# Top-k attention and two expert layers: the second head's keys stored with their last 64 in front

## Chip, cores and metric

The kernel runs on one core of a Trainium2 chip. The time is the device time of one execution in microseconds: 2257.2 us, the median of three runs of the kernel before (2256.66 to 2257.63).

## What is computed

```
scores = q @ k.T / sqrt(64)              # batch 4, heads 8, 576 queries, 576 keys, head size 64
mask   = scores >= 32nd largest of the row
attn   = softmax over the kept scores
x      = attn @ v                        # then laid out as [2304, 512]
x      = ((x @ w1) * (x @ w2)) @ w3 @ w_out
P      = exp(x @ w_gate - max), 8 rounds of row and column normalization
out    = sum over 8 experts e of P[:, e] * (relu(x @ m1[e]) @ m2[e])
```

All of it is float32. Matrix products run on operands that are split into a high and a low part.

## The kernel before

576 keys are four blocks of 128 (S4 = 512) and a rest of 64 (SR). Attention runs in the first third of the time, the expert layers in the rest; the change touches attention alone. Between the attention work, products of the first expert layer (L663, L691) are put in as filler for TensorE.

**Visits and steps.** A visit is one batch, one pair of heads and a range of query blocks; there are 28, numbered from 0. In all but the first batch each head pair has two visits, of two query blocks each. Attention goes in 72 steps of about 10 us. A normal step takes one query block of both heads of the pair (j = 0 is the first head, j = 1 the second): 64 of them. Eight tail steps take the 64 last queries of both heads, for two head pairs at once; there j is the head pair.

**A step's stations.** They are spread over four consecutive steps by an order written out by hand (`ORDERS`, one letter group for each operation): scores (`st_scores`, S0 and S1, L306), a top-32 search on VectorE and GpSimd, thresholding and exponential on ScalarE, normalization on GpSimd, transposes (`st_trans`, R0 and R1: four at L415 and one at L416 for each j), a copy of the transposed weights from the PSUM tile `tx` into `et` (L418, ScalarE), and the product with v (`st_av`, A, L444). Rows 512 to 575 of the keys go through the fifth transpose; it turns the columns 448 to 575 of one head, and v's tile `vn` has zeros for the 64 keys that come a second time. `P` in the order takes one piece of the preparation of the next visit, `F` a share of the filler.

**Preparation of a visit** (`prep_list`). Queries and keys come in from HBM, are transposed on TensorE (L229), copied into `kt` or `qt` (L145, ScalarE; one buffer each), split into parts (L245 ScalarE, L246 GpSimd), and put together for the scores by DMAs from one place of SBUF to another (`prep_stack`): the keys into `kst` (two buffers; for each head one DMA of 64 partitions by 2 by 576 at L258 and two of 64 by 576 at L260, six in all), the queries into `qst` (two buffers; L266 blocks, L268 the last 64). The next visit's copy into `kt` (L145) has to wait for all DMAs that read `kt`.

**SP's queue.** All these DMAs, the loads of v (`load_v`, L135 and L138), of k and q (L125, L127) and the stores of the expert layer (L698, L700) are issued by SyncE in the order of the program; an issue that waits holds up all behind it. In most visits the order is: keys into `kst`, v, queries into `qst`, next loads.

Of the kernel before, what the change touches and what calls it, by code (L numbers as in the profile page):

```python
# [7 lines left out]
F32 = mybir.dt.float32  # L8
# [10 lines left out]
def kernel(  # L19
# [14 lines left out]
    nc = tc.nc  # L34
# [66 lines left out]
    tx = aps.tile([128, 1024], F32, name="tx")  # L101
    vn_t = [ap1.tile([128, 2 * R + 2, D], F32, name=f"vn{i}") for i in range(2)]
    qst_t = [ap1.tile([128, 2 * S4 + 256], F32R, name=f"qst{i}") for i in range(2)]
# [27 lines left out]
    def load_v(p):  # L131
        b, hp = visits[p][:2]
        t = vn_t[p % 2]
        for i in range(2):
            nc.sync.dma_start(t[:, R * i:R * i + R, 0:D],  # L135
                              v[b, 2 * hp + i, 0:S4, :].rearrange("(p r) d -> p r d", r=R))
        for i in range(2):
            nc.sync.dma_start(t[64:128, 2 * R + i, 0:D], v[b, 2 * hp + i, S4:S, :])  # L138

# [27 lines left out]
    def prep_first():  # L167
# [8 lines left out]
        for n in range(2):  # L176
            copy(kst[0, n][:, :, S4:S], pt[:, 256 + 128 * n:384 + 128 * n].rearrange("p (h r) -> p h r", h=2), nc.vector)

    def prep_group(p, nm, g, eng=None, flip=False):
# [22 lines left out]
        else:  # L202
# [6 lines left out]
            if body:  # L209
                copy(dst[:, body[0] // R, 0:S4], pt, eng)  # L210
            if tail:
                copy(dst[:, :, S4:S], pt[:, w:w + 128].rearrange("p (h r) -> p h r", h=2), eng)

# [34 lines left out]
    def prep_stack(p, nm):  # L248
# [3 lines left out]
        if nm == "k":  # L252
            ks = ap1.tile([128, 2, 2, S], F32R, name="kst", tag="kst", bufs=2)
            for n in range(2):
                kst[p, n] = ks[:, n]
            for h in range(2):
                x = hl[64 * h:64 * h + 64]
                nc.sync.dma_start(ks.bitcast(F32)[0:64, :, h], x)  # L258
                for a in range(2):
                    nc.sync.dma_start(ks.bitcast(F32)[64:128, 1 - a, h], x[:, a])  # L260
            return
# [32 lines left out]
    def st_scores(st, j):  # L294
# [9 lines left out]
        for n, (lhs, hh, part) in enumerate(terms):  # L304
            for e in range(2):
                nc.tensor.matmul(ps[:, e, 0:SH], lhs, kst[p, part][:, hh, SH * e:SH * e + SH],  # L306
                                 start=(n == 0), stop=(n == len(terms) - 1))
        if j == 0:
# [102 lines left out]
    def st_trans(st, j):  # L411
        e = e_sb[st][:, j]
        ps = tx
        for c in range(R):
            nc.tensor.transpose(ps[:, 128 * c:128 * c + 128], e[:, 128 * c:128 * c + 128], ident)  # L415
        nc.tensor.transpose(ps[:, S4:S4 + 128], e[:, S - 128:S], ident)  # L416
        et = ap1.tile([128, (R + 1) * 128], F32, name="et", tag="et", bufs=2)
        nc.scalar.activation(et, ps[:, 0:(R + 1) * 128], AF.Copy)  # L418
        et_sb[st, j] = et
        if j:  # L420
            e_sb.pop(st)

    def st_av(st):
# [3 lines left out]
        if steps1[st][0][1] is None:  # L427
            for j in range(2):
                p = steps1[st][j][0]
                for c in range(R + 1):  # L430
                    for hh in range(2):
                        nc.tensor.matmul(ps[64 * hh:64 * hh + 64, 64 * j:64 * j + 64],
                                         vn_t[p % 2][:, R * hh + c if c < R else 2 * R + hh],
                                         et[j][:, 128 * c + 64 * hh:128 * c + 64 * hh + 64],
                                         start=(c == 0), stop=(c == R))
# [6 lines left out]
        for c in range(R + 1):  # L442
            for hh in range(2):
                nc.tensor.matmul(ps[64 * hh:64 * hh + 64, 0:128],  # L444
                                 vn_t[p % 2][:, R * hh + c if c < R else 2 * R + hh],
                                 et[hh][:, 128 * c:128 * c + 128], start=(c == 0), stop=(c == R))
        b, hp = visits[p][:2]
# [1206 lines left out]
```

## Time and profile before

| | |
|---|---|
| median of three runs | 2257.2 us |
| the profiled execution: time, span | 2257.63 us, 2255.8 us |
| mean granted TensorE clock | 0.984 |
| busy share of the span: PE, DVE, ACT, POOL | 97%, 79%, 54%, 67% |
| instructions of PE and of ACT | 13521, 2708 |

PE is TensorE's matmuls (transposes among them), PEld its weight loads, DVE VectorE, ACT ScalarE, POOL GpSimd, SP SyncE, and SPq SP's queue of DMA issues. L415 is line 415 of the kernel. In a timeline a row has its start in us from the start of the span, its duration, engine, line and operation, the tile that is written and what is read; x4 means four instructions that run after and into one another, and what stands in brackets is the idle time of the engine before the row and what ended it, by the profile. Ends of matmuls are modelled; the distance from start to start is the better measure of what one costs. A wait for several semaphores is put down to the one that came last by the profile; where the engine named had long been done, it was another, often a DMA.

### The profile page before, as it was taken

The page shows a single profiled execution, that of the slowest core. Times are in us where ns is not written, and L with a number is a line of the kernel's source. Part 1 is how long each engine was busy: PE and PEld are TensorE (multiplying, and loading weights), DVE is VectorE, ACT ScalarE, POOL GpSimd, SP SyncE. Part 2 cuts the span into 40 slices and gives each one's busy share as a digit, 9 for nine tenths or more (in the row PEclk, how much of TensorE's full clock was granted, in tenths as well). Part 3 has the DMA queues.
Part 4 walks back from the last instruction along what each step waited for, and adds up shares of the span by engine and source line. Part 5 has one row for each costly group of instructions (what it writes and reads, how often), then busy time and mean ns, then how long its engine had stood idle before and what let it go on. Part 6 is the DMA issues. An engine that isn't in the chain of part 4 may idle for free.

```text
span 2255.8 us, 42437 instructions
## 1 busy us (share of the span) xinstructions
PE 2186.6 (97%) x13521; PEld 2021.9 (90%) x13521; DVE 1774.2 (79%) x4396; ACT 1220.0 (54%) x2708; POOL 1515.3 (67%) x1828
## 2 busy tenths in 40 slices
PE   5897999999999999999999999999999999999999
PEld 4554898998888999999999899999999999999999
DVE  8999999999999557777777767777777677777776
ACT  7999778877777544444444344444444433333332
POOL 6889877767776257787778667777777544444443
PEclk6998999999999999999999999999999999999999
DMA  6545444544542177788778898888888987887885
GB/s 191 154 139 135 105 105 113 124 102 103 122 112 53 60 250 241 270 301 290 248 250 295 274 319 275 277 274 280 276 279 266 349 274 252 259 258 256 260 256 161
DMA packets 356078, 485.45 MB, mean 215 GB/s; under 512 B 95152, under 2 KB 166032, under 8 KB 355856
## 3 DMA queue, kind: packets, MB, share of 16 engines
q1 hardware_dynamic: 354320, 480.71, 67.7%
q8 instruction: 108, 1.77, 0.3%
q10 hardware_dynamic: 1536, 2.03, 0.3%
q14 instruction: 114, 0.93, 0.1%
HBM read 309.48 MB, written 132.43 MB: 196 GB/s over the span
## 4 chain that ended last, share of the span: by engine, by line
PE 82%; DVE 6%; POOL 4%; ACT 4%; DMA 2%; SPq 2%; issue 1%; ACTq 0%; POOLq 0%; DVEq 0%
PE l1ps L1219 30%; PE y L1518 20%; PE y L1278 12%; PE abps L663 8%; PE x2ps L691 3%; PE sps L306 2%; PE tx L444 2%; DVE tkv L355 2%; PE tx L415 2%; POOL low L344 1%; DVE rest L360 1%; DMA kst<-kt 1%; DVE G L517 1%; ACT s_sb L396 1%; PE x2ps L689 1%
## 5 line engine op out<-in xcount | busy, mean ns | idle before, releaser
L1219 PE MATMUL l1ps<-xB,wa 128*128 128x384 f32 x2688 | 540.6, 338 | 1.0 <-DVE tm_u L1448 0.5
L1518 PE MATMUL y<-h,v 128*128 128x384 f32 x2640 | 531.6, 337 | 0.2
L1219 PEld LDWEIGHTS l1ps<-xB,wa 128*128 128x128 f32 x2688 | 475.1, 188 | 3.4 <-DVE tm_u L1448 2.3
L1518 PEld LDWEIGHTS y<-h,v 128*128 128x128 f32 x2640 | 467.6, 188 | 0.9 <-DVE h L1455 0.8
L1455 POOL TENSOR_TENSOR h<-tm_t,h 128x384 fp32r<-128x384 f32 x192 | 195.9, 1021 | 245.4 <-ACT h L1454 239.3
L1529 DVE TENSOR_TENSOR Mc<-y,Mc 128x384 f32<-128x384 f32 x424 | 234.5, 553 | 139.2 <-PE y L1518 139.0
L1278 PE MATMUL y<-wb,hh 128*128 128x512 f32 x768 | 270.4, 394 | 0.0
L1219 PE MATMUL l1ps<-xAh,wa 128*128 128x384 f32 x896 | 260.6, 338 | 0.0
L1024 POOL TENSOR_TENSOR wa<-ws,wa 128x256 fp32r<-128x256 f32 x217 | 164.8, 762 | 98.6 <-ACT wa L1023 94.0
L1287 DVE SCALAR_TENSOR_TENSOR acc<-y,P,acc 128x512 f32<-128x512 f32 x168 | 126.0, 750 | 98.8 <-PE y L1278 96.3
L1455 POOL TENSOR_TENSOR h<-tm_b,h 128x384 fp32r<-128x384 f32 x128 | 133.5, 1048 | 87.1 <-ACT h L1454 72.4
L1454 ACT ACTIVATE h<-tm_t 128x384 fp32r<-128x384 f32 x192 | 99.5, 519 | 152.9 <-DVE tm_t L1493 148.9
L332 POOL TENSOR_TENSOR low<-s_sb 128x288 int32<-128x288 int32 x144 | 117.8, 818 | 95.9 <-ACT s_sb L310 94.0
L1244 ACT ACTIVATE hh<-l1ps 128x384 fp32r<-128x384 f32 x128 | 63.0, 492 | 211.8 <-DVE l1ps L1240 120.5
L355 DVE MAX8 tkv<-rest 128x8 f32<-128x288 f32 x432 | 175.1, 447 | 0.0
L1219 PEld LDWEIGHTS l1ps<-xAh,wa 128*128 128x128 f32 x896 | 164.8, 188 | 7.8 <-issue 0.5
L1278 PEld LDWEIGHTS y<-wb,hh 128*128 128x128 f32 x768 | 144.0, 188 | 24.6
L306 PE MATMUL sps<-kst,qst 128*128 128x288 f32 x640 | 128.8, 329 | 32.5 <-DVE top L339 31.3
L1219 PE MATMUL l1ps<-xAl,wa 128*128 128x384 f32 x448 | 150.5, 336 | 0.0
L1278 PE MATMUL y<-wb,hl 128*128 128x512 f32 x384 | 149.5, 389 | 0.0
L306 PEld LDWEIGHTS sps<-kst,qst 128*128 128x128 f32 x640 | 98.8, 199 | 56.1 <-DVE top L339 44.8
L1454 ACT ACTIVATE h<-tm_b 128x384 fp32r<-128x384 f32 x128 | 66.4, 521 | 135.5 <-DVE tm_b L1451 129.8
(223 smaller groups left out, 5321.2 us busy)
## 6 DMA issues: line engine op xcount, KB each, us to landing
wa<-wk SPq DMA_DIRECT2D x448, 256.0 KB, 3.5
v<-vk SPq DMA_DIRECT2D x343, 256.0 KB, 3.9
wk<-wa SPq DMA_DIRECT2D x224, 256.0 KB, 3.0
vk<-v SPq DMA_DIRECT2D x105, 256.0 KB, 2.8
ws<-in_moe_w_dram SPq DMA_DIRECT2D x35, 512.0 KB, 5.1
vk<-sp SPq DMA_DIRECT2D x68, 256.0 KB, 3.4
raw<-in_moe_w_dram SPq DMA_DIRECT2D x32, 512.0 KB, 4.1
ws<-in_moe_w_dram SPq DMA_DIRECT2D x128, 128.0 KB, 2.7
```

Source lines behind the costliest of these rows:

```text
L306: nc.tensor.matmul(ps[:, e, 0:SH], lhs, kst[p, part][:, hh, SH * e:SH * e + SH], start=(n == 0), stop=(n == len(terms) - 1))
L332: nc.gpsimd.tensor_tensor(low_sb[st][:, j].bitcast(I32), x[:, 0:SH], x[:, SH:S], ALU.add)
L355: nc.vector.max(vt[:, j, c:c + 8], x[:, j])
L663: nc.tensor.matmul(ps[:, 0:n], lhs, rhs[:, c, 0:n], start=(m == 0), stop=(m == 3 * KD - 1))
L1024: eng.tensor_tensor(t[:, 1], st[:, c], t[:, 0].bitcast(F32), ALU.subtract)
L1219: nc.tensor.matmul(ps, lhs[:, kc], rhs[:, kc], start=(first and k_ == 0), stop=(k_ == 3 * KH - 1), skip_group_check=True)
L1278: nc.tensor.matmul(ps, lhs[:, m, h, o:o + 128], rhs[:, m], start=(k_ == 0), stop=(k_ == 5))
L1287: nc.vector.scalar_tensor_tensor(a, ps, P[:, i, e:e + 1], a, op0=ALU.mult, op1=ALU.add)
L1454: nc.scalar.activation(h[k][:, 0], src, AF.Copy)
L1455: low = lambda: eng.tensor_tensor(h[k][:, 1], src, h[k][:, 0].bitcast(F32), ALU.subtract)
L1518: nc.tensor.matmul(ps, w[:, a, 128 * j:128 * j + 128], h[:, b], start=(first and q_ == 0), stop=(q_ == 5), skip_group_check=True)
L1529: nc.vector.tensor_tensor(m, ps, m, ALU.add)
```

## The change

The second head's keys are stored with keys 512 to 575 in front of keys 0 to 511. In a normal step the last 64 columns of the first head's weights and the first 64 of the second head's then lie side by side, and one transpose turns both: R0 has four transposes, R1 five. `vn` gets the first head's last 64 rows of v in partitions 0 to 63 for this, and a third tile with the same rows in partitions 64 to 127 for the tail steps, which takes one more DMA a visit. `prep_stack` stores the second head's keys in two ranges: six DMAs where there were three. In tail steps, where both heads stand in one row, the scores of the second head are put back in the old order by cutting its second matmul in two (224 and 64 columns), ten transposes stay, and the copy of j = 0 is in two pieces. `et` is one tile for each j.

```diff
--- before.py
+++ after.py
@@ -99,7 +99,7 @@
     nat = {}
     xT = [ap1.tile([128, KD, S], F32, name=f"xT{i}") for i in range(2)]
     tx = aps.tile([128, 1024], F32, name="tx")
-    vn_t = [ap1.tile([128, 2 * R + 2, D], F32, name=f"vn{i}") for i in range(2)]
+    vn_t = [ap1.tile([128, 2 * R + 3, D], F32, name=f"vn{i}") for i in range(2)]
     qst_t = [ap1.tile([128, 2 * S4 + 256], F32R, name=f"qst{i}") for i in range(2)]
     for i in range(2):
         nc.gpsimd.memset(vn_t[i][:, 2 * R:, :], 0.0)
@@ -135,7 +135,8 @@
             nc.sync.dma_start(t[:, R * i:R * i + R, 0:D],
                               v[b, 2 * hp + i, 0:S4, :].rearrange("(p r) d -> p r d", r=R))
         for i in range(2):
-            nc.sync.dma_start(t[64:128, 2 * R + i, 0:D], v[b, 2 * hp + i, S4:S, :])
+            nc.sync.dma_start(t[64 * i:64 * i + 64, 2 * R + i, 0:D], v[b, 2 * hp + i, S4:S, :])
+        nc.sync.dma_start(t[64:128, 2 * R + 2, 0:D], v[b, 2 * hp, S4:S, :])
 
     kst = {}
     split = {}
@@ -174,7 +175,7 @@
         copy(qst_t[0][:, 0:2 * S4].rearrange("p (h s) -> p h s", h=2)[:, :, 0:128],
              pt[:, 0:256].rearrange("p (h s) -> p h s", h=2), None, scale)
         for n in range(2):
-            copy(kst[0, n][:, :, S4:S], pt[:, 256 + 128 * n:384 + 128 * n].rearrange("p (h r) -> p h r", h=2), nc.vector)
+            copy(kst[0, n].rearrange("p h s -> p (h s)")[:, S4:S4 + 128], pt[:, 256 + 128 * n:384 + 128 * n], nc.vector)
 
     def prep_group(p, nm, g, eng=None, flip=False):
 
@@ -207,9 +208,8 @@
                     kst[p, m] = ks[:, m]
             dst = kst[p, n]
             if body:
-                copy(dst[:, body[0] // R, 0:S4], pt, eng)
-            if tail:
-                copy(dst[:, :, S4:S], pt[:, w:w + 128].rearrange("p (h r) -> p h r", h=2), eng)
+                h = body[0] // R
+                copy(dst[:, h, SR * h:S4 + SR * h], pt, eng)
 
     kgroups = [list(range(R)), list(range(R, 2 * R)), [2 * R]]
 
@@ -255,9 +255,11 @@
                 kst[p, n] = ks[:, n]
             for h in range(2):
                 x = hl[64 * h:64 * h + 64]
-                nc.sync.dma_start(ks.bitcast(F32)[0:64, :, h], x)
-                for a in range(2):
-                    nc.sync.dma_start(ks.bitcast(F32)[64:128, 1 - a, h], x[:, a])
+                for s0, s1, d0 in ((0, S4, SR), (S4, S, 0)) if h else ((0, S, 0),):
+                    d1 = d0 + s1 - s0
+                    nc.sync.dma_start(ks.bitcast(F32)[0:64, :, h, d0:d1], x[:, :, s0:s1])
+                    for a in range(2):
+                        nc.sync.dma_start(ks.bitcast(F32)[64:128, 1 - a, h, d0:d1], x[:, a, s0:s1])
             return
         for h in range(2):
             for a in range(2):
@@ -302,9 +304,12 @@
             c0 = S4 * h + 128 * t
             terms = [(qs[:, c0:c0 + 128], h, part) for part in range(2)]
         for n, (lhs, hh, part) in enumerate(terms):
-            for e in range(2):
-                nc.tensor.matmul(ps[:, e, 0:SH], lhs, kst[p, part][:, hh, SH * e:SH * e + SH],
-                                 start=(n == 0), stop=(n == len(terms) - 1))
+            cuts = ((0, 0, SH, 0), (1, 0, SH, SH))
+            if h is None and hh:
+                cuts = ((0, 0, SH, SR), (1, 0, SH - SR, SH + SR), (1, SH - SR, SH, 0))
+            for e, c0, c1, k0 in cuts:
+                nc.tensor.matmul(ps[:, e, c0:c1], lhs, kst[p, part][:, hh, k0:k0 + c1 - c0],
+                                 start=(n == 0), stop=(n == len(terms) - 1), skip_group_check=True)
         if j == 0:
             s_sb[st] = ap1.tile([128, 2, S], F32, name="s_sb", tag="s_sb", bufs=4)
         nc.scalar.activation(s_sb[st][:, j].rearrange("p (a b) -> p a b", a=2), ps[:, :, 0:SH], AF.Copy)
@@ -411,11 +416,22 @@
     def st_trans(st, j):
         e = e_sb[st][:, j]
         ps = tx
+        both = steps1[st][0][1] is not None
+        c0 = SR if both and j else 0
         for c in range(R):
-            nc.tensor.transpose(ps[:, 128 * c:128 * c + 128], e[:, 128 * c:128 * c + 128], ident)
-        nc.tensor.transpose(ps[:, S4:S4 + 128], e[:, S - 128:S], ident)
-        et = ap1.tile([128, (R + 1) * 128], F32, name="et", tag="et", bufs=2)
-        nc.scalar.activation(et, ps[:, 0:(R + 1) * 128], AF.Copy)
+            nc.tensor.transpose(ps[:, 128 * c:128 * c + 128], e[:, c0 + 128 * c:c0 + 128 * c + 128], ident)
+        w = S4
+        if j or not both:
+            ends = e_sb[st].rearrange("p j s -> p (j s)")[:, S4:S4 + 128] if both else e[:, S - 128:S]
+            nc.tensor.transpose(ps[:, w:w + 128], ends, ident)
+            w += 128
+        et = ap1.tile([128, (R + j) * 128], F32, name=f"et{j}", tag=f"et{j}", bufs=1)
+        w = min(w, (R + j) * 128)
+        nc.scalar.activation(et[:, 0:w], ps[:, 0:w], AF.Copy)
+        et = [et[:, 128 * c:128 * c + 128] for c in range(R + j)]
+        if not j and not both:
+            nc.scalar.activation(e[:, 0:128], ps[:, S4:S4 + 128], AF.Copy)
+            et.append(e[:, 0:128])
         et_sb[st, j] = et
         if j:
             e_sb.pop(st)
@@ -430,8 +446,8 @@
                 for c in range(R + 1):
                     for hh in range(2):
                         nc.tensor.matmul(ps[64 * hh:64 * hh + 64, 64 * j:64 * j + 64],
-                                         vn_t[p % 2][:, R * hh + c if c < R else 2 * R + hh],
-                                         et[j][:, 128 * c + 64 * hh:128 * c + 64 * hh + 64],
+                                         vn_t[p % 2][:, R * hh + c if c < R else 2 * R + 2 - hh],
+                                         et[j][c][:, 64 * hh:64 * hh + 64],
                                          start=(c == 0), stop=(c == R))
             for j in range(2):
                 b, hp = visits[steps1[st][j][0]][:2]
@@ -443,7 +459,7 @@
             for hh in range(2):
                 nc.tensor.matmul(ps[64 * hh:64 * hh + 64, 0:128],
                                  vn_t[p % 2][:, R * hh + c if c < R else 2 * R + hh],
-                                 et[hh][:, 128 * c:128 * c + 128], start=(c == 0), stop=(c == R))
+                                 et[hh if c < R else 1][c], start=(c == 0), stop=(c == R))
         b, hp = visits[p][:2]
         xev.append(lambda: nc.scalar.activation(xT[b % 2][:, hp, 128 * t:128 * t + 128], ps[:, 0:128], AF.Copy))
 
```

## Rows read from the trace of the kernel before

**Rows 1.** Windows: length; busy us (x) PE, PEld, DVE, ACT, POOL; clock; DMA; GB/s.

```profile
40.00:240.00 200.00, 164.72 (x984) 109.58 (x984) 191.47 (x629) 189.84 (x387) 172.80 (x204) 0.88 0.52 139
240.00:720.00 480.00, 472.50 (x3921) 425.54 (x3920) 448.18 (x1666) 378.90 (x871) 348.67 (x508) 1.00 0.45 107
```

**Rows 2.** Groups by shape, 240 to 720 us: busy, mean ns, idle before.

```profile
L415 PE MATMUL tx<-ident,s_sb 128*128 128x128 f32 x402 | 60.6, 273 | 0.6 <-ACT et L418 0.5
...
L418 ACT ACTIVATE et<-tx 128x640 f32<-128x640 f32 x100 | 69.9, 699 | 11.1 <-PE tx L416 10.3
```

**Rows 3.** Timeline of PE, 404 to 407 us: start, us, what.

```profile
404.48 0.60 PE L415 MATMUL tx<-ident,s_sb 128*128 128x128 f32 x4
404.91 0.27 PE L416 MATMUL tx<-ident,s_sb 128*128 128x128 f32 x1
...
405.73 0.69 PE L306 MATMUL sps<-kst,qst 128*128 128x288 f32 x4
406.26 0.28 PE L663 MATMUL abps<-xh,w2h 128*128 128x256 f32 x1
```

**Rows 4.** Chain that ended last, 240 to 720 us: start, us, what.

```profile
278.69 3.84 DMA kst<-kt
287.35 1.83 DMA qst<-qt
```

**Rows 5.** Timeline of SP, ACT and PE, 274 to 287 us.

```profile
274.88 0.62 SPq L258 DMA_DIRECT2D kst<-kt  x1
...
277.95 1.97 SPq L260 DMA_DIRECT2D kst<-kt  x2
...
281.18 1.13 SPq L138 DMA_DIRECT2D vn<-in_v_dram  x2
...
282.40 1.07 SPq L266 DMA_DIRECT2D qst<-qt  x1
282.61 0.60 ACT L145 ACTIVATE kt<-pt 128x512 f32<-128x512 f32 x1 [0.57 <-DMA kst<-kt]
283.52 0.59 SPq L268 DMA_DIRECT2D qst<-qt  x1
283.85 1.31 PE L444 MATMUL tx<-et,vn 128*64 128x128 f32 x20 [0.18 <-ACT et L418]
284.20 0.55 SPq L266 DMA_DIRECT2D qst<-qt  x1
286.29 0.76 PE L306 MATMUL sps<-kst,qst 128*128 128x288 f32 x4
```

**Rows 6.** Timeline of SP, DVE and PE, 589 to 593 us.

```profile
589.71 2.40 SPq L266 DMA_DIRECT2D qst<-qt  x4
590.84 0.44 DVE L339 TENSOR_TENSOR top<-sps,s_sb 128x288 f32<-128x288 f32 x1
592.38 0.76 PE L306 MATMUL sps<-kst,qst 128*128 128x288 f32 x4 [0.38 <-DVE tkv L355]
```

**Rows 7.** Timeline of SP and PE: first and last of 21 visits.

```profile
263.85 2.46 SPq L266 DMA_DIRECT2D qst<-qt  x4
267.50 0.70 PE L306 MATMUL sps<-kst,qst 128*128 128x288 f32 x4
...
700.05 1.56 SPq L268 DMA_DIRECT2D qst<-qt  x1
704.10 1.23 PE L306 MATMUL sps<-kst,qst 128*128 128x288 f32 x8
```

**Rows 8.** DMA issues, 240 to 720 us: count, size, median us to landing.

```profile
kst<-kt SPq DMA_DIRECT2D x84, 144.0 KB, 3.8
...
qst<-qt SPq DMA_DIRECT2D x87, 64.0 KB, 2.0
...
qst<-qt SPq DMA_DIRECT2D x48, 16.0 KB, 1.8
```

**Rows 9.** Waits, 240 to 720 us: total us, times, longest.

```profile
ACT kt L145 <- DMA kst<-kt: 12.4, 9, 2.7
PEld tx L444 <- ACT et L418: 10.6, 12, 2.2
ACT kt L145 <- PE sps L306: 5.0, 3, 1.8
```

**Rows 10.** Waits of SP's queue, 240 to 720 us.

```profile
SPq L127 <- PE tx L416: 62.9, 17, 6.7
SPq L266 <- POOL qt L246: 5.6, 3, 4.0
```

## Prediction

> **What bounds the kernel now.** I read the windows first, then the groups, the chain and the waits of the attention stage, and last the timelines of SP and PE. The change acts on attention alone. In 40 to 240 us VectorE (191.5 of 200 us) and ScalarE (189.8) are the full engines and PE has 35 us of gaps; in 240 to 720 us PE is busy for 472.5 of 480 us at the full clock, VectorE for 448 [rows 1]. So a transpose less is worth its price on PE in the second stretch, 54 of the 72 steps, and next to nothing in the first.
>
> PE's 7.5 idle us in that stretch are not spread evenly. The chain there runs through `kst<-kt` and `qst<-qt` transfers [rows 4]: the preparation of the next visit arrives only just in time. Two places show it. ScalarE waits for the `kst` DMAs before it may overwrite `kt` (12.4 us in 9 waits, and 3 more put down to PE that end in the same way), and behind that copy stands the copy of `et`, for which the product with v waits [rows 9]; the `kt` copy at 282.61 starts after a wait, and PE at 283.85 after a gap of 0.18 [rows 5]. And the first scores of a visit need `qst`: the `qst` DMAs needed for them start at 282.40 and 284.20 [rows 5], a landing takes 2.0 us [rows 8], so 286.2, and the scores start at 286.29. There the queries are late already [rows 6]: DMAs from 589.71, 0.60 apart, the second landed at 592.3, and PE stands still for 0.38 until 592.38. The row names VectorE, but all that the scores need of it is L339, done at 591.28.
>
> **What the change removes.** 48 of the 54 steps are normal and lose one transpose. One has a duration of 273 ns [rows 2], but four of them start 0.43 us apart from the fifth [rows 3], 0.108 each: 48 x 0.108 = 5.2 us of PE. The Trainium skill (TensorE: Matmul & The Clock Gate, PE-mode transpose) gives about 275 ns for one in a kernel, which would make it 13.2 us; the trace has this as the duration, and not as the distance, and a sum by that figure would be 8 us lower. The copy of `et` for j = 0 shrinks from 640 to 512 columns, 699 ns [rows 2] to about 600 (a 512-column copy at 282.61 [rows 5]): 0.1 us a step. In 240 to 720 us ScalarE has 101 us idle and this is worth nothing; before 240 us at most 16 x 0.1 = 1.6, of which I take nothing, since VectorE is as full there.
>
> **What it adds on PE.** In a tail step the second head's 288-column matmul becomes 224 and 64: 4 more matmuls a step, 24 in the PE-bound stretch. A 288-column one takes 0.13 [rows 3]. The columns are the same, so an extra one costs between nothing and a transpose's 0.108; I take 0.03, 0.7 us in all (range 0 to 2.6). The two-piece copy of j = 0 in tail steps costs ScalarE some 0.2 us in six steps, beside its idle time.
>
> **What it adds on SP.** Three more `kst` issues a visit and one more of v. The nearest rows are pieces of 64 partitions by 64 elements: an L268 issue holds the queue for 0.59 and the next starts 0.68 later, elsewhere 0.63 [rows 5]; two L138 take 1.13. So the queries' DMAs, next in the queue, start 3 x 0.63 + 0.55 = 2.44 us later, or 1.89 in the five visits without a v load in between. Below, 1.5 would do if an issue is short while the DMA engines are still behind with the keys; above, the fourth to sixth `kst` issues are held up to 1.0 each by that backlog (two L260 in 1.97 [rows 5]), so 3.5. Bytes are the same, and so I take the transfers as no longer.
>
> What stands behind these issues on SP: `qst`, then the next loads of k and q, then stores. Those later ones have cover: SP waits 62.9 us for the transposes of the `ends` tile [rows 10]. `qst` has none: in nearly all visits SP goes from keys through v to queries without a pause, and its waits at L266 are 3, of 5.6 us in all [rows 10].
>
> **The sum of the waits.** For the 21 visits of the stretch (first and last: [rows 7]) I take the start of the scores less the landing of the `qst` DMAs that they need (first head's two, or all eight where the visit begins with a tail step). In visits with v in between the spare time is 1.06, 0.13, 1.46, 3.45, 0.97, 0.93, 0.18, 0.23, 1.86, 0, 0.69, 0.13, 0.57, 0.84, 1.77, 1.30; in the others 1.62, 1.67, 2.78, 3.02, 1.58. What is later than the spare time is PE's wait, since scores stand in PE's order ahead of all filler: 15 x 2.44 - 12.1 = 24.5, and 0.27 + 0.22 + 0.31 = 0.8; less 1.8 us in three visits in which SP waits between keys and queries anyway: 23.5.
>
> The `kt` copy waits for the last of nine DMAs. The last one is issued 1.9 us later, but a small one lands after 1.8 and not 3.8 [rows 8]; with the engines' backlog I take 0.8 us later (range 0.3 to 1.5). Of 15 visits in which the product with v starts within 0.75 us of the copy of `et`, each loses 0.8 less what it has spare: 9.3 us. It falls on PE before the same visit's scores, which then wait less, so the two don't add; where it is the larger it brings 2.9 more. Against that, in seven visits SP is held for 0.5 to 1.2 us by the DMA backlog between keys and queries (the 1.07 at L266 [rows 5]), 5.4 us that the longer queue would partly cover: I take off half, 2.7. Of the transposes' 5.2 us, 0.13 a visit in 18 visits fall between the keys' issue and the scores and only lengthen the wait: 2.3.
>
> Sum: -5.2 + 0.7 + 23.5 + 2.9 - 2.7 + 2.3 = +21.5. PE's lost time is lost, since all later attention work keeps its order behind it, and after 720 us nothing is changed. The profiled execution took 2257.6 (span 2255.8 and 1.8 around it), 0.4 over the median: 2279.1 for it, 2279 as the forecast. If the clock fell in the waits it would be more; PE was less busy in the stretch before.
>
> **Rivals.**
> *The extra issues are hidden, and PE's saving shows.* SP has over 60 us of waits in the stretch [rows 10], and the bytes are unchanged. It would be 2257.2 - 5.2 + 0.7 = 2252.7, or 2251 with ScalarE's share. Against it: the pauses lie ahead of the keys, not between keys and queries. The Trainium skill (DMA: Bandwidth & Descriptors, Issuing engines are not separate DMA queues) says that the time to start a DMA is usually small beside the DMA; by that this rival would hold. The trace disagrees here: 0.59 of issue for a landing of 1.8 us.
> *Only the copy into `kt` is late.* If `qst` lands earlier than it seems (the row of 592.38 names VectorE, after all), 9.3 - 5.2 + 0.7 + 1 = +6: 2263; with 0.3 us of delay it would be no change, 2255. For it: this wait stands in the waits by its name [rows 9].
> *The DMA backlog holds each extra issue for 1.0 to 1.3.* The queries are 3.6 to 4.4 us late, and the same sum gives 50 to 60 us of waits: 2305. For it: the third and sixth `kst` issue are stretched already. Against: the v issues right behind are not.
> *The transposes are not on the path at all* belongs to the first 240 us only.
>
> **How the numbers follow.** The late queries 0.62, of their own 2268 to 2296 (1.5 to 3.0 us a visit, with or without the cover of the backlog); only the copy 0.14 (half of it slower, half no change); hidden 0.11 (mostly faster, part of it no change); backlog 0.08; the rest, 0.05, no change by offsetting. A measurement here can tell about 0.2%, 4.5 us, from no change. Faster 0.09; within 0.2% 0.14; slower 0.77. The range takes in the copy's case and most of the late queries': 2258 to 2298.
>
> **What would show it.** Right: SP rows with nine `kst` issues and then v and `qst`, the latter 2 to 2.5 us after where they stood relative to the first `kst` issue; PE gaps of 1 to 2 us ahead of L306's counterpart at a visit's first scores, none elsewhere; PE busy some 20 us less than the span of the stretch, which grows from 480 to about 500 us. The `kt` copy's waits longer by about 1 us. Wrong: PE gaps as before, with the stretch shorter by 4 or 5 us (hidden); gaps ahead of the product with v alone (copy); `kst` issues of over 1 us each (backlog). A tail step that is longer by more than 0.3 us on PE would show the cut matmuls dearer than I took them; step distances of normal steps that shrink by 0.1 us between waits show the transposes right.

## The result, and the profile after

The changed kernel takes 2286.3 us (median of 4 runs, 2284.3 to 2287.3) where the kernel before takes 2257.1 (4 runs, 2256.7 to 2257.6): a ratio of 1.0127, 95% interval 1.0115 to 1.0139. The forecast was 2279, with a range of 2258 to 2298. Its sign, its range and its causes hold, and its sum of the waits comes out 2 us too high; what it lacks is the clock, which it gave no price, and part of the cost of the cut matmuls.

The profiled execution took 2287.3 us with a span of 2285.4 (before: 2257.6 and 2255.8). The attention stage, up to the first matmul of the second layer, ends at 827.2 us in place of 797.3: +29.9, which is all of it. Windows of the kernel after, columns as in [rows 1]; the last three are stretches that I picked for their clock:

```profile
40.00:240.00 200.00, 164.88 (x977) 110.03 (x975) 190.73 (x629) 189.16 (x389) 173.63 (x204) 0.85 0.51 142
240.00:720.00 480.00, 450.84 (x3662) 401.99 (x3662) 424.26 (x1572) 357.79 (x836) 333.31 (x483) 0.99 0.45 105
460.00:470.00 10.00, 7.89 (x63) 6.14 (x60) 6.85 (x26) 5.33 (x14) 4.80 (x8) 0.90 0.52 129
632.00:638.00 6.00, 5.07 (x23) 4.68 (x21) 4.78 (x20) 2.96 (x6) 2.90 (x6) 0.50 0.45 112
730.00:740.00 10.00, 7.99 (x60) 7.21 (x59) 6.79 (x26) 3.68 (x9) 3.16 (x5) 0.83 0.13 35
```

The first stretch is as it was. In the second PE is busy for 450.8 of 480 us, where it was 472.5, and no other engine is busier for it: all wait. And the clock, 1.00 throughout before, now falls to 0.50 (1.2 GHz of 2.4) for 3 to 7 us at three places, at 468, 632 and 734 us, each behind a wait of PE of 1.6 to 2.1 us.

Groups by shape, 240 to 720 us, as [rows 2]:

```profile
L422 PE MATMUL tx<-ident,s_sb 128*128 128x128 f32 x384 | 58.3, 275 | 0.9 <-POOL low L349 0.4 <-POOL s_sb L414 0.2
...
L430 ACT ACTIVATE et<-tx 128x640 f32<-128x640 f32 x48 | 33.4, 697 | 1.5 <-PE tx L426 1.1
L430 ACT ACTIVATE et<-tx 128x512 f32<-128x512 f32 x48 | 28.7, 599 | 8.3 <-PE tx L422 7.9
...
L426 PE MATMUL tx<-ident,s_sb 128*128 128x128 f32 x53 | 14.5, 273 | 0.0
```

The 100 copies of 640 columns of [rows 2] are 48 of 640 and 48 of 512 now, the latter 0.1 us shorter, and there are 53 fifth transposes where five to a step's head would make 96. So the change does what it says.

PE's idle time sits in two lines. Groups of PE, 240 to 750 us (busy, mean ns, idle before, what ended it):

```profile
L311 PE MATMUL sps<-kst,qst 128*128 128x288 f32 (+2 forms) x472 | 86.2, 309 | 15.5 <-DMA qst<-qt 9.8 <-DVE rest L365 2.9 <-DVE tkv L360 2.6
...
L460 PE MATMUL tx<-et,vn 128*64 128x128 f32 x900 | 60.1, 280 | 14.8 <-ACT et L430 14.4
```

In the kernel before the same two rows have 0.5 us (scores) and 6.3 us (product with v) in the idle column. The waits that answer to [rows 9], same stretch:

```profile
PEld tx L460 <- ACT et L430: 20.0, 16, 2.5
ACT kt L146 <- DMA kst<-kt: 18.0, 9, 3.0
...
PE sps L311 <- DMA qst<-qt: 9.8, 10, 2.0
ACT kt L146 <- PE sps L311: 8.3, 4, 2.7
```

PE waits for the copy of `et` 20.0 us in place of 10.6, and ScalarE in front of the `kt` copy 18.0 and 8.3 in place of 12.4 and 5.0. The wait for `qst` is new, and by its own name. SP's wait that answers to [rows 10] shows that the later loads had their cover; it shrinks from 62.9:

```profile
SPq L127 <- PE tx L426: 53.4, 17, 6.3
```

One visit shows both. Timeline of SP, ACT and PE, 276 to 290 us, as [rows 5]:

```profile
276.62 0.62 SPq L260 DMA_DIRECT2D kst<-kt  x1
...
281.55 0.62 SPq L260 DMA_DIRECT2D kst<-kt  x1
282.21 1.39 SPq L262 DMA_DIRECT2D kst<-kt  x2
...
284.97 0.60 ACT L146 ACTIVATE kt<-pt 128x512 f32<-128x512 f32 x1 [1.71 <-DMA kst<-kt]
286.00 0.59 SPq L139 DMA_DIRECT2D vn<-in_v_dram  x1
286.22 1.31 PE L460 MATMUL tx<-et,vn 128*64 128x128 f32 x20 [0.97 <-ACT et L430]
286.68 0.55 SPq L268 DMA_DIRECT2D qst<-qt  x1
...
290.04 0.77 PE L311 MATMUL sps<-kst,qst 128*128 128x288 f32 x4 [1.45 <-DVE tkv L360]
```

The last three key stores (from 281.55) end at 283.60; the first query goes out at 286.68, 10.06 after the first key store, where it was 7.52. ScalarE stands for 1.71 before the `kt` copy at 284.97, so `et` is late and PE stands for 0.97 before the product with v. Then it stands again, 1.45, before the scores: the row names VectorE, as at [rows 6], but the third query DMA, which these scores need, starts at 287.96, and with the 2.0 us of a landing [rows 8] that is 290.0. The two waits come one behind the other in one visit, and they do not add: the scores' start is set by the landing, and without the 0.97 us ahead of the product with v PE would have come to the scores earlier and waited there for as much longer.

### The profile page after: what moved, and what is told of

It is laid out like the page before. It is cut to its first block, busy times and chain, and to the rows that moved or that the text cites. A ratio compares the mean times of both kernels' runs of the same rounds, so it can differ in the third digit from the quotient of the medians.

```text
span 2285.4 us, 42556 instructions
## 1 busy us (share of the span) xinstructions
PE 2192.4 (96%) x13489; PEld 2024.7 (89%) x13489; DVE 1775.7 (78%) x4396; ACT 1216.8 (53%) x2716; POOL 1517.2 (66%) x1828
## 2 busy tenths in 40 slices
DMA packets 366527, 485.92 MB, mean 213 GB/s; under 512 B 105600, under 2 KB 176480, under 8 KB 366304
## 4 chain that ended last, share of the span: by engine, by line
PE 74%; DVE 6%; POOL 5%; SPq 5%; ACT 4%; DMA 2%; issue 2%; ACTq 0%; POOLq 0%; DVEq 0%
PE l1ps L1235 30%; PE y L1534 20%; PE y L1294 12%; PE abps L679 4%; SPq L262 2%; DVE tkv L360 2%; PE x2ps L707 2%; PE sps L311 2%; POOL low L349 1%; DVE rest L365 1%; PE tx L460 1%; SPq L260 1%; PE tx L422 1%; POOL low L337 1%; DMA kst<-kt 1%
## 5 line engine op out<-in xcount | busy, mean ns | idle before, releaser
L311 PE MATMUL sps<-kst,qst 128*128 128x288 f32 (+2 forms) x672 | 134.3, 329 | 48.8 <-DVE top L344 32.6
L311 PEld LDWEIGHTS sps<-kst,qst 128*128 128x128 f32 x672 | 104.5, 203 | 75.7 <-DVE top L344 46.4
```

Of the source, the lines that this page charges most:

```text
L311: nc.tensor.matmul(ps[:, e, c0:c1], lhs, kst[p, part][:, hh, k0:k0 + c1 - c0], start=(n == 0), stop=(n == len(terms) - 1), skip_group_chec ...
```

## The experiments

Twelve kernels. For each I read four things in the stretch from 240 us to the end of attention. Two are from SP's timeline, over the 21 or 22 visits: **q**, from the start of the first key store to the start of the first query DMA (mean), and **k**, from the first key store to the landing of the last (median). **Waits** are the idle column of the two PE rows shown above, scores and product with v. **Clock** is the sum over windows of 10 us of (1 - granted clock) x 10 us. The time is the difference of the medians to the kernel before run beside it.

```
                       stores  q us  k us  scores   v    clock  time
before                   6     7.65  7.87    0.5   6.3    0       -
after                    9     9.99  8.36   15.5  14.8    6.8   +29.2
split only               9     9.45  8.40    8.3  13.2    0     +18.7
queue only               6+3   9.57  7.80   16.6   4.9    3.4   +20.8
nine only                6     7.76  7.93    1.5   3.7    0      -6.3
cut only                 6     as before     0.8   5.9    1.7    +1.7
third v late             9     9.55  8.33    9.8  14.3    0     +18.5
all v late               9     8.39  8.52    6.3  14.4    5.1   +15.6
nine and queue           6+3   as queue     16.1   5.6    1.7   +15.4
rotated copy             6     7.75  7.75    1.2   6.6    0      +2.9
six merged               6     9.29  8.18   12.7  10.5    0     +17.3
six merged, third v late 6     8.96  8.00    5.6   9.1    1.7    +9.9
four merged              4     7.71  8.05    1.4   7.3    0      +0.9
tails from GpSimd        6+3   7.80  7.81    3.0   6.9    3.4   +16.9
```

**1. The split stores alone.**

```diff
-                nc.sync.dma_start(ks.bitcast(F32)[0:64, :, h], x)
-                for a in range(2):
-                    nc.sync.dma_start(ks.bitcast(F32)[64:128, 1 - a, h], x[:, a])
+                for s0, s1 in ((0, S4), (S4, S)) if h else ((0, S),):
+                    nc.sync.dma_start(ks.bitcast(F32)[0:64, :, h, s0:s1], x[:, :, s0:s1])
+                    for a in range(2):
+                        nc.sync.dma_start(ks.bitcast(F32)[64:128, 1 - a, h, s0:s1], x[:, a, s0:s1])
```

> The kernel before, but the second head's keys are stored in two ranges in place of one, three more stores of a visit (nine in place of six), in the same layout; TensorE's work is the kernel before's, ten transposes a step and no matmul cut. Theory (the stores on SP's queue make the loss: the queries are issued about 1.9 us later in a visit, the last key store lands 0.6 us later): TensorE waits at the first scores of a visit and at the products with v as in the changed kernel, 2270 to 2290 us, and the transposes' 5 us aren't there to be taken off. Rival (the loss is TensorE's own, by the cut matmuls and the order of the transposes): 2257 us, as before, with the idle time ahead of the scores at 0.5 us.

2276.2 us, ratio 1.0089 (1.0075 to 1.0103): in the theory's range, and far from the rival's 2257. With PE's work untouched, three more stores make two thirds of the loss.

**2. Queue time without late keys.**

```diff
             ... (behind the six key stores)
+            for n in range(3):
+                nc.sync.dma_start(scr[3 * p + n], ident[0:64, 0:64])
```

> The kernel before with three more transfers of 16 KB in each visit, from a constant to a scratch in memory, issued by SP between the keys' stores and the queries; keys, queries and TensorE's work are the kernel before's, and the keys' stores are issued at their old times. Theory (lateness of the queries and lateness of the transposed keys are two prices): only the queries are late, so the idle time ahead of the first scores comes to about 15 us and that ahead of the product with v stays near 6; 2270 to 2278 us. Rival (the later release of the keys' buffer makes the loss): 2257 to 2260 us, with no idle time ahead of the scores.

2278.3 us, 1.0095 (1.0080 to 1.0111): at the top of the theory. The queries are 1.9 us later and the keys land when they did. The two PE rows of this kernel:

```profile
L309 PE MATMUL sps<-kst,qst 128*128 128x288 f32 x452 | 84.4, 312 | 16.6 <-DVE tkv L358 8.0 <-DMA qst<-qt 6.7 <-DVE rest L363 2.0
...
L447 PE MATMUL tx<-et,vn 128*64 128x128 f32 x920 | 60.5, 278 | 4.9 <-ACT et L421 4.7
```

All the new idle time is ahead of the scores, none ahead of the product with v (6.3 before). So late queries alone cost that much, and the waits ahead of the product with v have another cause. The two rows have 21.5 us together, and in experiment 1, with the queries nearly as late (9.45) and the keys late too, they also have 21.5: where the queries are late, the late keys move idle time from the scores to the product with v and add none.

**3. The transposes' gain alone.**

```diff
-        nc.tensor.transpose(ps[:, S4:S4 + 128], e[:, S - 128:S], ident)
+        full = j or steps1[st][0][1] is None
+        if full:
+            nc.tensor.transpose(ps[:, S4:S4 + 128], e[:, S - 128:S], ident)
...
-                                 et[hh][:, 128 * c:128 * c + 128], start=(c == 0), stop=(c == R))
+                                 et[hh if c < R else 1][:, 128 * c:128 * c + 128], start=(c == 0), stop=(c == R))
```

> The kernel before with nine transposes in the normal steps: the fifth transpose of one head is left out, so the product of its last 64 keys with v is not the reference's; the stores, the queue and the scores are the kernel before's. Theory: 48 steps become shorter by 0.108 us each, 2252 us. Rival (TensorE then waits for the eviction of the transposed weights, so that the saving is swallowed): 2255 to 2257 us.

2251.2 us, 0.9975 (0.9966 to 0.9985), that is 3.4 to 7.7 us less. The forecast's 5.2 lies in the middle; the idle time stays at 7.1 us (7.5 before).

**4. The cut matmuls alone.**

```diff
-            for e in range(2):
...
+            cuts = ((0, 0, SH, 0), (1, 0, SH, SH))
+            if h is None and hh:
+                cuts = ((0, 0, SH, 0), (1, 0, SH - SR, SH), (1, SH - SR, SH, S - SR))
+            for e, c0, c1, k0 in cuts:
```

> The kernel before with the second scores matmul of the second head in the tail steps cut in two, 224 and 64 columns, 24 cuts in all; nothing else is changed. Theory (read from the changed kernel's records: the matmul behind a 64-column one takes 84 ns more, beside 8 ns for the cut itself): 24 x 0.09 = +2.2 us, 2259.3 us. Rival (the prediction's price, 24 x 0.03 = 0.7 us): 2257.8 us.

2259.1 us, 1.0006 (0.9997 to 1.0015): this can't tell the two prices apart, and its profiled execution has 1.7 us of fallen clock, which alone would explain it. The rows do better. A stretch of score matmuls in a tail step has two cuts, and the row behind the second one is longer too (0.39 in place of 0.31), so the time to read is that from the first score matmul to the second row behind the stretch:

```profile
310.52 1.32 PE L309 MATMUL sps<-kst,qst 128*128 128x288 f32 x10
311.67 0.39 PE L666 MATMUL abps<-xh,w1h 128*128 128x320 f32 x1
311.90 0.31 PE L666 MATMUL abps<-xl,w1h 128*128 128x320 f32 x1
```

Here it is 1.38 us, and 1.22 in the kernel before (310.98 to 312.20). The 11 stretches without a wait are 0.14 to 0.20 us longer, 0.167 in the mean: 0.084 a cut, and 2.0 us for 24 of them. The theory's price, 2.2, holds against the prediction's 0.7.

**5. The added v store behind the queries.**

```diff
-        nc.sync.dma_start(t[64:128, 2 * R + 2, 0:D], v[b, 2 * hp, S4:S, :])
+        v3.append(lambda: nc.sync.dma_start(t[64:128, 2 * R + 2, 0:D], v[b, 2 * hp, S4:S, :]))
...
         some_prep(9)
+        while v3:
+            v3.pop(0)()
```

> The changed kernel with the third store of v's last rows (the one that the change adds) issued at the end of its step, behind the queries, in place of ahead of them; no byte more or less. The split alone cost 18.7 us, the transposes alone gave 6.3, the cuts alone cost 1.7, which adds to 14.1 where the change cost 29.2. Theory (the rest is that store's 0.6 us in the queue ahead of the queries, in most visits): 2271 to 2274 us, the parts' sum. Rival (in the changed kernel the queries set the pace of a visit, so that what the transposes save is swallowed by the waits): 2277 to 2280 us. Second rival (the rest is the fallen clock or the cut matmuls in company): 2283 to 2286 us.

2275.7 us, 1.0084 (1.0069 to 1.0100), between the theory's range and the first rival's. One store of 16 KB, 0.59 us of issue and 0.4 in the mean of q, costs 10.6 us where it stands in the change. In the profiled executions 4.6 of that are idle time and 6.8 the clock, which does not fall here. Against the parts' sum, 14.1, 4 us are missing: with late keys and late queries together, part of what the transposes save is waited away (26.6 us of idle time in all, 23.3 in the first experiment).

**6. All of v behind the queries.**

```diff
-            loads.setdefault(last[p - 2] + 3, []).append(lambda p=p: load_v(p))
+            vloads.setdefault(last[p - 2] + 3, []).append(lambda p=p: load_v(p))
...
         some_prep(9)
+        for fn in vloads.get(s, []):
+            fn()
```

> The changed kernel with all five stores of v issued at the end of their step, behind the queries. The queries are then issued about where the kernel before issued them (nine key stores, no v: 5.6 us of queue in place of 3.7 + 1.9), while the last key store still lands 0.6 us late. Theory (the queries' lateness is the loss): the waits at the first scores go, the waits ahead of the product with v stay, 2257 to 2266 us. Rival (the keys' buffer, released later, makes a good part of it by itself): 2268 to 2278 us.

2272.8 us, 1.0073 (1.0060 to 1.0087): the time is in the rival's range. The edit does not take v out of the way everywhere, though. In the five visits that had no v between keys and queries it now stands there, and their queries go out 5 us later than in the kernel before; SP's timeline of one, behind the last key store:

```profile
328.17 1.89 SPq L135 DMA_DIRECT2D vn<-in_v_dram  x2
...
331.97 0.54 SPq L268 DMA_DIRECT2D qst<-qt  x1
```

Four of these five hold 6.2 of the 6.3 us of waits ahead of the scores. In the other 16 the queries go out 0.6 us earlier than before, and these waits are gone, as the theory had it. The keys land as late as in the change, and the waits ahead of the product with v stay whole:

```profile
441.56 0.60 ACT L146 ACTIVATE kt<-pt 128x512 f32<-128x512 f32 x1 [1.42 <-issue]
442.05 0.70 ACT L430 ACTIVATE et<-tx 128x640 f32<-128x640 f32 x1
442.80 1.31 PE L460 MATMUL tx<-et,vn 128*64 128x128 f32 x20 [2.01 <-ACT et L430]
```

This is a timeline of ACT and PE in that kernel. ScalarE stands in front of the `kt` copy (the row names no DMA, but the last key store of this visit landed at 441.3), the copy of `et` is behind it in its order, and PE stands for 2.0 us. Such waits of over 0.25 us ahead of the product with v number 7 in the kernel before and 13 here. So late keys by themselves bring 8 us of idle time.

**7. Both the gain and the late queries.**

```diff
... (the edits of 2 and 3 in one kernel)
```

> The kernel before with both earlier edits at once: three transfers of 16 KB between the keys and the queries (alone: +20.8 us) and nine transposes in the normal steps, with the last 64 keys of one head left out of the product with v (alone: -6.3 us). Theory 1 (they add, TensorE still sets the pace): 2272 us. Theory 2 (with the queries late, the queue and not TensorE sets the time of a visit, and the shorter steps only wait longer): 2277 to 2279 us, with 5 us more idle time ahead of the scores than with the transfers alone.

2272.6 us, 1.0068 (1.0055 to 1.0082): theory 1 to the microsecond. Late queries alone do not swallow what the transposes save (20.8 - 15.4 = 5.4, of which 1.7 is the clock).

**8. Nine transposes without new stores.**

```diff
+        cut = S4 // 2 if h == 1 else SH
...
+        o = SR * (h == 1)
+        nc.scalar.activation(s_sb[st][:, j, o:o + 2 * cut].rearrange("p (a b) -> p a b", a=2), ps[:, :, 0:cut], AF.Copy)
+        if o:
+            nc.scalar.activation(s_sb[st][:, j, 0:SR], ps[:, 1, cut:cut + SR], AF.Copy)
... (and the stores as in the kernel before)
```

> Nine transposes without the change's stores: the keys lie and are stored as in the kernel before (six stores, no cut matmuls); ScalarE's copy of the second head's scores into SBUF goes in two pieces, 512 columns and then the last 64, and puts these in front; v's third store is made only in the visits with tail steps and a step later. If the changed kernel's loss is the queue ahead of the queries, this one keeps the transposes' gain: 2251 to 2255 us, with ScalarE 0.1 to 0.2 us busier in a step. Rival (ScalarE's added piece delays the eviction of the transposed weights, which TensorE waits for): 2257 to 2264 us.

2260.1 us, 1.0012 (1.0003 to 1.0020): not the gain, and not by the rival's way, for the waits ahead of the product with v are as before (6.6). Windows of this kernel:

```profile
40.00:240.00 200.00, 158.85 (x965) 106.32 (x963) 190.91 (x619) 188.91 (x403) 173.40 (x203) 0.88 0.49 139
240.00:720.00 480.00, 468.35 (x3865) 419.88 (x3866) 454.15 (x1671) 375.50 (x922) 356.82 (x509) 1.00 0.46 108
```

Up to 240 us ScalarE is the full engine, as in [rows 1], and it now does 403 instructions in the same busy time while PE gets 5.9 us less done. The 41st of the 144 score copies starts at 228.6 us in place of 226.3. After 240 us 4.5 us of idle time come on, about half of them ahead of the transposes and the scores (idle 12.0 in all, 7.5 before), and use up the rest.

**9 to 11. Merged stores.** The two stores into the swapped half are one, with the planes reversed: nine become six (9, and 10 with the added v store late as well), and in the kernel before six become four (11).

```diff
-                    for a in range(2):
-                        nc.sync.dma_start(ks.bitcast(F32)[64:128, 1 - a, h, d0:d1], x[:, a, s0:s1])
+                    nc.sync.dma_start(ks.bitcast(F32)[64:128, ::-1, h, d0:d1], x[:, :, s0:s1])
```

> The changed kernel with the two stores that put a range's high and low parts into the other half's rows merged into one (the destination's two planes taken in reverse order): six key stores a visit, three ranges, with the same bytes at the same places. Theory (the number of stores that SP issues one behind the other makes both latenesses): the queries late by v's 0.6 us alone, the keys' buffer free as before, so the transposes' -6.3, the cuts' +1.7 and a rest of score waits, 2253 to 2259 us. Rival (a merged store moves twice the bytes and lands later, so that the keys' buffer is free no earlier): waits ahead of the product with v as in the changed kernel, 2262 to 2272 us.

> As the changed kernel with six merged key stores, and v's added store issued behind the queries: nothing of the change is left in the queue ahead of the queries. Theory: 2251 to 2255 us, faster than both kernels, with about 7 us of idle time in TensorE's stretch as in the kernel before. Rival (the merged stores land later): 2262 to 2270 us.

> The kernel before with the same merge alone: four key stores a visit in place of six, ten transposes. Theory (the queue's price also works downwards): the queries go out 1.2 us or more earlier and the keys' buffer comes free earlier, so the 6.3 us that TensorE waits ahead of the product with v shrink: 2251 to 2256 us. Rival (the kernel before has no wait at the scores, and its waits ahead of the product with v come from elsewhere or from the landing of the bytes): 2256 to 2260 us.

2275.3 us, 1.0080 (1.0066 to 1.0093); 2268.0, 1.0042 (1.0030 to 1.0055); 2258.9, 1.0004 (0.9995 to 1.0012). The first is over both ranges, the other two lie in the rivals'. Their reason, a later landing, holds in small measure (k is 8.0 to 8.2); the larger part is that six merged stores hold SP for 6.3 us where nine hold it for 7.1, so that, with v's added store, the queries are still 1.64 us late. SP's timeline, first six merged, then four:

```profile
594.47 0.62 SPq L260 DMA_DIRECT2D kst<-kt  x1
595.13 0.61 SPq L261 DMA_DIRECT2D kst<-kt  x1
595.79 0.90 SPq L260 DMA_DIRECT2D kst<-kt  x1
596.73 1.51 SPq L261 DMA_DIRECT2D kst<-kt  x1
598.29 1.13 SPq L260 DMA_DIRECT2D kst<-kt  x1
599.46 1.29 SPq L261 DMA_DIRECT2D kst<-kt  x1
```

```profile
582.83 0.90 SPq L258 DMA_DIRECT2D kst<-kt  x1
583.77 1.53 SPq L259 DMA_DIRECT2D kst<-kt  x1
585.39 2.59 SPq L135 DMA_DIRECT2D vn<-in_v_dram  x2
```

These times go from the first key store to the end of the last issue, means of 21 visits; the six of the kernel before take 5.1 and the four 3.8. With four stores the keys are issued 1.3 us sooner, and v's two, 1.02 in the same visit of the kernel before, then take 2.59: q is 7.71, as before. A merged store moves 128 rows (64 partitions by two planes), as many as the two that it replaces; the page counts 356,078 packets before and 355,213 with four stores, 366,527 after and 365,230 with six. So the number of stores fell, rows and packets hardly did, and SP's time fell by less than the stores. Rows alone don't set it either: the store at 598.29 is not merged, and the same store of 128 rows and 32 KB took 0.62 in the changed kernel (281.55), where no merged ones stood ahead of it. What stretches it is open. The Trainium skill (Perfetto Trace Analysis, What "DMA-bound" means) has it that a DMA's window on the issuing engine's sequencer is the making of its descriptors, not the movement of the data. As to bytes the trace agrees: in the changed kernel a key store of 288 KB (276.62) and one of 32 KB (281.55) both hold SP for 0.62 us.

**12. The small stores from another queue.**

```diff
-                    nc.sync.dma_start(ks.bitcast(F32)[0:64, :, h, d0:d1], x[:, :, s0:s1])
+                    q_ = nc.gpsimd if h and not d0 else nc.sync
+                    q_.dma_start(ks.bitcast(F32)[0:64, :, h, d0:d1], x[:, :, s0:s1])
... (and v's added store as in 5)
```

> The changed kernel with the three added key stores (the second head's last 64 keys) issued by GpSimd in place of SP, and v's added store behind the queries: SP's queue ahead of the queries is the kernel before's again, six key stores of 144 and 128 KB, and the same bytes and packets move as in the changed kernel. Theory (SP's queue makes the loss): idle time ahead of the product with v 6 to 8 us, ahead of the scores 0 to 3, 2252 to 2257 us. Rival (the added packets in the shared transfer engines hold back the landing of the keys, whichever queue they come from): 2264 to 2272 us with 9 to 14 us ahead of the product with v, as with six merged stores. Second rival (GpSimd, 20 us busier or more by issuing, delays the top-k work that the steps wait for): 2258 to 2265 us with the waits on GpSimd and VectorE.

2274.2 us, 1.0071 (1.0057 to 1.0085). The theory's mechanism holds and its time does not: q and k are back at 7.80 and 7.81, the waits at 3.0 and 6.9, with the change's bytes all moved (in 360,912 packets, 5,615 fewer than in the changed kernel, so that the rival of the packets is weakened and not excluded). The second rival takes it back, dearer than I had it. Groups of this kernel, PE then GpSimd:

```profile
L425 PE MATMUL tx<-ident,s_sb 128*128 128x128 f32 x416 | 64.0, 277 | 8.4 <-POOL s_sb L417 6.6 <-ACT et L433 1.0 <-POOL low L352 0.4
```

```profile
L265 POOL DMA_DIRECT2D kst<-kt x44 | 22.7, 521 | 0.0
...
L263 POOL DMA_DIRECT2D kst<-kt x21 | 14.2, 675 | 0.0
```

GpSimd issues for 37 us, and PE waits 8.4 us ahead of the transposes (0.6 before), most of it for GpSimd's scaling of the weights. The 41st score copy starts 6.6 us late already, in the stretch where VectorE and ScalarE are full [rows 1]. The Trainium skill (Perfetto Trace Analysis, DMA Optimizations) says that spreading DMAs over several engines may help where the making of descriptors is the limit; here that took the waits on SP's queue away and cost more on GpSimd.

## Why the prediction was right, point by point

- **Late queries: right, in mechanism and lateness.** 2.44 us were forecast; the mean is 9.99 - 7.65 = 2.34. The price was 23.5 less 2.7; 1.92 us alone cost 20.8 (experiment 2), of which 16.1 are waits ahead of the scores and 3.4 clock. In the changed kernel itself this wait grows by 15.0 us; the rest is taken ahead of the product with v, as the prediction had it. The landing of a query takes what it took (2.0 and 1.8 us), so it is the issue that is late and not the transfer.
- **The `kt` copy: right, in its overlap with the queries too.** The last key store goes out 2.5 us later (1.9 was taken) and lands 0.5 later (0.8 was taken; the small stores land after 2.2 and 2.8 us, not 1.8), and PE's wait ahead of the product with v grows by 8.5 us where the prediction counted 9.3. It grows as much with the queries nearly back in place (6) and by 0.6 us at most with the keys in time (2, 7 and 12): two causes. But "the two don't add" holds: alone, late keys bring 8 us of idle time and late queries 16; together they bring 16 (1, against 2 with the same lateness of the queries), or 19 with nine transposes (5), where late queries alone bring 17 (7). On top of the late queries the late keys cost 0 to 2.3 us; 2.9 was forecast. "None elsewhere", of the gaps, fails, and it didn't fit the prediction's own 9.3.
- **The sum of the waits: 2 us too high.** 23.5 + 2.9 - 2.7 + 2.3 = 26.0 us were forecast, and the idle time grew by 23.8.
- **The clock: named, not priced.** "If the clock fell in the waits it would be more": it fell in three places, 6.8 us. It does not go by the sum of idle time alone: 26.6 us in experiment 5 without a fall, 22.5 in experiment 6 with 5.1 us of it. This term, put at nothing, is the largest part of what the forecast falls short by.
- **The transposes: right.** -5.2 forecast, -6.3 measured (3.4 to 7.7). In the profiled executions 4.7 of it lie behind the 47th score copy, at 258 us; the 1.5 ahead of that are in part the difference between executions, for experiments 1, 2 and 4, which change no transposes, are 0.7 to 0.8 us early there too. The Trainium skill's figure for one (TensorE: Matmul & The Clock Gate, PE-mode transpose) is the duration in the records again, 275 ns; as a price it would have made 13.2, and no run gives that.
- **What waits swallow of it (2.3): half right.** Some 1 us with late queries alone (idle 24.3 in 7, 23.4 in 2), about 4 us where the keys are late as well (5 against its parts).
- **The cuts: 0.7 forecast, about 2.0** by the rows (4), inside the term's range of 0 to 2.6.
- **The rivals.** Hidden issues (2252.7) and the backlog that holds each for over 1 us (2305) fell: the added issues mostly take 0.59 to 0.62 us. "Only the copy" fell as the sole cause, but as a part it is real.

The sum by rows: idle +23.8, clock +6.8, cuts +2.0, transposes -5.2, together 27.4 of the 29.9 by which attention ends later. The 2.5 that are left have a likely place. PE's windows from the 47th score copy to the end of attention, the kernel before and then split only (length, PE's busy time, clock, DMA):

```profile
258.47:797.32 538.85, 531.35 (x4332) 1.00 0.43 104
257.68:814.88 557.20, 533.93 (x4332) 1.00 0.41 100
```

The instructions and the clock are the same, and PE is busy for 2.6 us more: matmuls lie one into the other, and those around a wait less so (about the wait of 1.14 at 316.1 in the changed kernel they count 0.29 and 0.21 us, elsewhere 0.13), so that a wait costs somewhat more than its idle column. That this is the whole of the changed kernel's rest is not shown. Where the clock fell is known for profiled executions alone; the mean clock of the other three, 0.982, does not tell it, since experiment 5 has 0.982 without a fall in this stretch.

No version here that computes everything beats the kernel before. The one that took nine transposes and paid nothing leaves a product out (3); each way to pay for them, SP, ScalarE or GpSimd, cost more than 5 us.

## What to carry to other kernels

A DMA issue has a price for everything behind it on its queue: before adding one, find what is next in that queue and how much time it has to spare. Here that was under 1 us in 10 of 16 visits, so four small issues cost more than five times what the transposes gave. Give each buffer that comes free later its own sum, and then ask what ends the second wait: here the queries' landing did, so that a wait ahead of it in the same visit cost little more. And a kernel that begins to wait can lose its clock as well.

## What the runs showed of the hardware that I had not expected

- The time that a store holds SP followed neither its bytes nor its rows alone: 288 KB took 0.62 us as a visit's first, 32 KB in 128 rows took 0.62 as the seventh of nine and 1.13 behind merged ones, 256 KB merged took 1.5; and what a shorter issue saved was taken back at the next transfers (v's pair, 2.59 us).
- A 64-column matmul makes the one behind it dearer: cutting 288 columns into 224 and 64 cost 0.084 us, nearly all of it in the row behind (experiment 4).
- GpSimd's issues count as busy in its row, 0.52 and 0.68 us each.
- The clock stood at 1.2 GHz in place of 2.4 from 632 to 638 us, with PE busy in 5.07 of these 6 us, behind a wait of 2.0 at 628.7; a like wait of 2.0 at 545.1 was followed by no fall.
